# Decode attention block: one head's output weights loaded on 8 partitions, the other seven regrouped, and the last values in two loads

## The chip, the cores and the metric

The kernel runs on one core of one Trainium2 chip. The time is the device time of one execution in microseconds (us). Three runs of the kernel before took 1311.50, 1311.68 and 1311.70 us; their median is 1311.68 us. One more execution was recorded by the hardware profiler and took 1311.62 us, of which its profile spans 1309.6 us from the first instruction to the last; the other 2.0 us lie around that span.

## The reference

One decode step for two sequences (B = 2) of width 512. A layer norm of `x` feeds two branches whose results are multiplied and added to `x`:

```python
xn = _layernorm(x)
q = (xn @ wq).reshape(B, 1, 32, 128)                 # 32 query heads
scores = einsum(q, k) * 128 ** -0.5                  # 8 key/value heads, 4 query heads on each,
o = softmax(scores) @ v                              # 32768 cached positions, all float32
s = o.reshape(B, 1, 4096) @ wo                       # output weights: 4096 x 512
g = silu(relu(xn @ w1 + b1) ** 2 @ w2 + b2)          # 512 -> 1792 -> 512
out = x + s * g
```

The two caches hold 2 x 8 x 32768 x 128 float32 numbers each, 268 MB each. `wq` and `wo` are 8.4 MB each, `w1` and `w2` 3.7 MB each. Everything is read once.

## The kernel before, in words

The 16 streams `s` are the pairs of a key/value head and a sequence (`s = 2 * hkv + b`). For each stream the keys come in two loads of 8 MB (`load_k`, L98) and the values in two loads of 8 MB (`load_v`, L103), each of 64 KB on every one of 128 partitions. Keys live in `kslots`, three slots of 4 MB (L134); values in `vbuf` (L135), 8 MB. Only the last but one value load goes to `kslots`, slots 0 and 1 (L105).

`scores` (L236) turns each quarter of a stream's keys with VectorE's 32x32 transposes into `kt` (L248) and multiplies it on TensorE (L253). `softmax` (L260) and `probs` (L283) make the probabilities `pT`. `values` (L308) multiplies one value load on TensorE into `o_ps` (L316), 32 matmuls of 512 columns, each of which the trace shows as two passes. After a stream's second value load ScalarE copies `o_ps` to `o_sb` (L323), TensorE adds up the four groups and scales (L327), and VectorE writes the four heads' column to `oT` (L328), which holds 128 elements of each head on 128 partitions.

All large loads are issued by SyncE in one fixed order, the list `loads` (L136 to L141). Every entry names the event after which it may be issued (`past`, `give`, `issue`); SyncE's queue is in order, so a load that waits for its buffer holds back all that follow. At the end of the list stand the last two value loads and then the output weights: `load_wo` (L120) fetches `wo` in four groups of eight heads (1024 rows, 2 MB). Partition p gets rows 8p to 8p + 7 of a group, 16 KB in one piece. Groups 0 and 1 go to `kslots` slot 2, groups 2 and 3 to slot 0. The last group comes in four loads, cut by row number on the partition: `PIECES` (L33) gives rows 0 to 3, 4 and 5, 6, and 7, which is 8, 4, 2 and 2 KB on each partition.

For this layout the attention result has to be spread so that partition p holds the elements that meet rows 8p to 8p + 7. For each pair of key/value heads the kernel multiplies `oT` with the selector `sele` on VectorE (`om`, L332), multiplies by the selector `selj` on TensorE (L335), and ScalarE copies the 128x8 result into `oW[:, i, :, b]` (L336). `oW` is kept 32 columns wide, of which two are used.

`project` (L395) then multiplies each row `j` of a group, in four matmuls of 128 columns (one for each quarter of the 512 outputs, on column groups of TensorE), into one accumulator `a_ps`. Its order is group 0, 1, 2, and then the pieces of group 3 (L401 to L404). Two VectorE instructions, the product with `gate` (L406) and the sum with `xe` (L407), and one store for each sequence (L409) end the program.

The work at the start that the change touches: VectorE builds the selectors from the identity with one TENSOR_REDUCE each (L166 to L177), GpSimd clears `oW` (L180), and the layer norm waits for `x` (L190 to L198).

Of the kernel before, what the change touches and what calls it, by code (L numbers as in the profile page):

```python
# [9 lines left out]
F32 = mybir.dt.float32  # L10
AF = mybir.ActivationFunctionType
ALU = mybir.AluOpType
AX = mybir.AxisListType

P = 128
# [12 lines left out]
CHUNK = P * RUN  # L28
# [1 line left out]
TS = (1, 0, 2, 3)  # L30
NT = 4
HALF = 64 * 128
PIECES = ((0, 4), (4, 6), (6, 7), (7, 8))  # L33


@with_exitstack
def gqa_decode_kernel(ctx: ExitStack, tc: tile.TileContext, x, kc, vc, wq, wo, w1, b1, w2, b2, out):
    nc = tc.nc
    B, _, D = x.shape
    _, HKV, SK, DH = kc.shape  # L40
    HQ = wq.shape[1] // DH
# [7 lines left out]
    DE = D // NG  # L49
    WG = 8  # L50
    NWG = HQ // WG
# [6 lines left out]
    const = ctx.enter_context(tc.tile_pool(name="const", bufs=1))  # L58
    ktpool = ctx.enter_context(tc.tile_pool(name="ktpool", bufs=8))
    work = ctx.enter_context(tc.tile_pool(name="work", bufs=2))  # L60
# [3 lines left out]
    def misc(name):  # L64
        return pms.tile([P, 512], F32, tag="ms", name=name)
# [16 lines left out]
    def rows(cache, s):  # L82
        hkv, b = divmod(s, B)
        return cache[b, hkv]
# [17 lines left out]

    def load_v(m):  # L103
        s, u = divmod(m, NCH)
        t = vbuf if m != NV - 2 else kslots[:, 0:2, :].rearrange("p i f -> p (i f)")  # L105
        nc.sync.dma_start(t, rows(vc, s)[u * CHUNK:(u + 1) * CHUNK].rearrange("(p r) d -> p (r d)", p=P))
        return t.rearrange("p (r d) -> p r d", d=DH)
# [9 lines left out]
        return t.rearrange("p (j e) -> p j e", j=FJ)  # L117


    def load_wo(i):  # L120
        if i % 2 == 0:
            wide[i // 2] = kslots[:, 2 - i].rearrange("p (i j e) -> p i j e", i=2, j=WG)
        t = wide[i // 2][:, i % 2]
        src = wo[i * WG * P:(i + 1) * WG * P, :].rearrange("(p j) e -> p j e", p=P)
        if i < NWG - 1:
            nc.sync.dma_start(t, src)
        else:
            for j0, j1 in PIECES:
                nc.sync.dma_start(t[:, j0:j1, :], src[:, j0:j1, :])  # L129
        return t  # L130

    wide = {}
    NK, NV = NS * NT, NS * NCH
    kslots = const.tile([P, 3, HALF], F32, name="kslots")  # L134
    vbuf = const.tile([P, 2 * HALF], F32, name="vbuf")  # L135
    loads = [(None, load_wq, 0), (None, load_half, 0), (None, load_half, 1), (("q", 0), load_w1, 0),  # L136
             (("s", 0), load_half, 2), (None, load_half, 3), (("q", 0), load_w2, 0)]
    for m in range(2, NV):
        loads += [(("s", 2 * m - 2), load_k, m), (("v", m - 3) if m > 2 else ("w", 1), load_v, m - 2)]
    loads += [(("s", NK - 2), load_v, NV - 2), (("v", NV - 3), load_v, NV - 1)]  # L140
    loads += [(("s", NK - 1), load_wo, 0), (("s", NK - 1), load_wo, 1), (("v", NV - 2), load_wo, 2), (("v", NV - 2), load_wo, 3)]  # L141
    past = {None}
    done = [0]

# [6 lines left out]
    def take(f, a):  # L151
        return tiles.pop((f, a))

    def give(*event):
        past.add(event)
        issue()
# [4 lines left out]
    ident = const.tile([P, P], F32, name="ident")  # L161
# [12 lines left out]
    selj = const.tile([P, WG], F32, name="selj")  # L174
    nc.vector.tensor_reduce(selj, ident.rearrange("p (e j) -> p j e", j=WG), axis=AX.X, op=ALU.add)
    sele = const.tile([P, P // WG], F32, name="sele")
    nc.vector.tensor_reduce(sele, ident.rearrange("p (e j) -> p e j", j=WG), axis=AX.X, op=ALU.add)  # L177
    oT = const.tile([P, HQ, B], F32, name="oT")
    oW = const.tile([P, NWG, WG, 32], F32, name="oW")
    nc.gpsimd.memset(oW, 0.0)  # L180
    sc = [pone.tile([P, 512], F32, tag=f"sc{i}", name=f"sc{i}") for i in range(NT)]
    o_ps = [pone.tile([P, 512], F32, tag=f"o{i}", name=f"o_ps{i}") for i in range(2)]
    for t in o_ps:
# [16 lines left out]
    t_ps = misc("xnT_ps")  # L200
# [6 lines left out]
    for d in range(ND):  # L207
        for f in range(2):
            for g in range(NG):
                cc = f * NG + g  # L210
                nc.tensor.matmul(sc[f][32 * g:32 * g + 32, :], xnT[:, d, 0:32], wqt[:, d, cc * 512:(cc + 1) * 512],  # L211
                                 start=(d == 0), stop=(d == ND - 1))
    give("q", 0)
    qT = const.tile([P, B, HKV, REP, 4], F32, name="qT")
    for f in range(2):
        for h in range(REP):
# [3 lines left out]
            t_ps = misc(f"qT_ps{f}_{h}")  # L220
            for e in range(4):
                nc.tensor.transpose(t_ps[:, e * P:(e + 1) * P], qr[:, e].rearrange("p a w -> p (a w)"), ident)  # L222
            v = t_ps.rearrange("p (e g y) -> p g e y", e=4, g=NG)
# [84 lines left out]
    def values(n):  # L308
        s, k = divmod(n, NCH)
        vt = take(load_v, n)  # L310
        o = o_ps[s % 2]
        for c in range(2):
            for i in range(NO // 4):
                for g in range(NG):
                    lo = (c * NG + g) * NO + 4 * i
                    nc.tensor.matmul(o[32 * g:32 * g + 16, :], pT[s][:, k, g, c, 4 * i:4 * i + 4, :].rearrange("p o h -> p (o h)"),  # L316
                                     vt[:, lo:lo + 4, :].rearrange("p o d -> p (o d)"),
                                     start=(k + c + i == 0), stop=(k == NCH - 1 and c == 1 and i == NO // 4 - 1))
        give("v", n)
        if k == NCH - 1:  # L320
            hkv, b = divmod(s, B)
            o_sb = work.tile([P, 512], F32, tag="o_sb", bufs=1, name=f"o_sb{s}")
            nc.scalar.copy(o_sb, o)  # L323
            t_ps = misc(f"oT_ps{s}")
            r4 = rs.pop(s)
            for i in range(4):
                nc.tensor.matmul(t_ps[:, :REP], o_sb[:, i * DH:(i + 1) * DH], r4[:, i, :], start=(i == 0), stop=(i == 3))  # L327
            nc.vector.tensor_copy(oT[:, hkv * REP:(hkv + 1) * REP, b], t_ps[:, :REP])  # L328
            if hkv % 2 == 1:
                i = hkv // 2  # L330
                m = work.tile([P, WG, P // WG], F32, tag="om", bufs=1, name=f"om{s}")
                nc.vector.tensor_mul(m, oT[:, i * WG:(i + 1) * WG, b:b + 1].to_broadcast([P, WG, P // WG]),  # L332
                                     sele[:, None, :].to_broadcast([P, WG, P // WG]))
                t_ps = misc(f"oW_ps{s}")
                nc.tensor.matmul(t_ps[:, :WG], m.rearrange("p h e -> p (h e)"), selj, start=True, stop=True)  # L335
                nc.scalar.copy(oW[:, i, :, b], t_ps[:, :WG])  # L336


# [34 lines left out]
    for n in range(NK):  # L373
        s, i = divmod(n, NT)
        if i == 0:
            set_q(s)
        scores(n)
        if n == 1:
            mlp_up()
        if n == 3:  # L380
            mlp_down()
        if i == 3:
            softmax(s)
        if n >= 5 and n % 2 == 1:
            values((n - 5) // 2)
        if i == 3:
            probs(s)
    values(NV - 2)
    values(NV - 1)


    a_ps = sc[0]
    wot = [take(load_wo, i) for i in range(NWG)]

    def project(i, j0, j1):  # L395
        for j in range(j0, j1):
            for g in range(NG):
                nc.tensor.matmul(a_ps[32 * g:32 * g + 32, :DE], oW[:, i, j, :], wot[i][:, j, g * DE:(g + 1) * DE],
                                 start=(i == 0 and j == 0), stop=(i == NWG - 1 and j == WG - 1))

    for i in range(NWG - 1):  # L401
        project(i, 0, WG)
    for j0, j1 in PIECES:
        project(NWG - 1, j0, j1)  # L404
    asb = work.tile([P, DE], F32, tag="e", bufs=1, name="a_sb")
    nc.vector.tensor_mul(asb, gate, a_ps[:, :DE])  # L406
    nc.vector.tensor_add(xe, asb, xe)  # L407
# [25 lines left out]
```

## Time and profile before

| What | Value |
|---|---|
| median of three runs | 1311.68 us |
| the profiled execution, and its span | 1311.62 us, 1309.6 us |
| mean granted TensorE clock | 0.841 of full speed |
| TensorE matmul busy, 4926 records | 885.4 us, 68% of the span |
| TensorE weight loads busy | 251.1 us, 19% |
| VectorE busy, 742 instructions | 648.8 us, 50% |
| ScalarE, GpSimd busy | 88.3 us, 15.1 us |
| read from HBM | 561.01 MB, 428 GB/s over the span |
| packets on queue q8, kind "instruction" | 38, 0.62 MB |
| last value load landed, as TensorE saw it | 1285.88 us |
| last of the output weights landed | 1305.55 us |

Busy time is summed over an engine's instructions. In the chain that ended last, each step is followed back to what released it, so a transfer that stands there includes its time in the queue. Besides the views, the trace holds one record for every DMA packet, with its start, duration, size and queue, but not which of the core's 16 DMA engines moved it. On one engine a packet starts 3 or 4 ns before the packet ahead of it ends, so the records can be strung into 16 chains. A load on 128 partitions puts eight packets on every chain, followed by one record of 4 bytes, the engine's completion count.

### The profile page before, as it was taken

Reading aid. Unit: us, or ns where it says so; the run is one execution under the profiler, and the core shown is the slowest. Engines: PE = TensorE matmul, PEld = TensorE weight load, DVE = VectorE, ACT = ScalarE, POOL = GpSimd, SP = SyncE. Lnnn points to the kernel's source line nnn. Section 1 sums busy time; section 2 is a strip of 40 time slices with the busy share of each in tenths; the row PEclk is TensorE's granted clock in tenths of the full one; section 3 lists DMA queues with packets and bytes.
Section 4 is the critical chain, followed back from the end, with each engine's and each line's share of the span. In section 5 each row is a group of like instructions: output and inputs, shape, how many; then the busy total and the mean of one; then the engine's idle time right before and its main releaser. Section 6 shows DMA issues by size and latency. Waiting matters only on the chain.

```text
span 1309.6 us, 11506 instructions
## 1 busy us (share of the span) xinstructions
PE 885.4 (68%) x4926; PEld 251.1 (19%) x4926; DVE 648.8 (50%) x742; ACT 88.3 (7%) x237; POOL 15.1 (1%) x76
## 2 busy tenths in 40 slices
PE   3867675658757567775657766566875756776575
PEld 1222121112212111121212211111221211112123
DVE  2855654435555344655435565443655534465410
ACT  0010010101001010000101001010000101000010
POOL 0000000000000000000000000000000000000000
PEclk9988877888878788877789978778987878888788
DMA  9999999999999999999999999999999999999997
GB/s 403 433 441 439 424 439 423 441 433 431 435 427 435 435 427 443 423 439 428 437 429 431 435 427 443 419 443 429 435 435 427 439 427 437 435 425 441 421 441 303
DMA packets 11040, 561.74 MB, mean 429 GB/s; under 512 B 1239, under 2 KB 1259, under 8 KB 1646
## 3 DMA queue, kind: packets, MB, share of 16 engines
q1 hardware_dynamic: 10952, 561.00, 99.2%
q8 instruction: 38, 0.62, 0.2%
q14 instruction: 12, 0.10, 0.0%
q10 hardware_dynamic: 38, 0.02, 0.0%
HBM read 561.01 MB, written 0.00 MB: 428 GB/s over the span
## 4 chain that ended last, share of the span: by engine, by line
DMA 74%; DVE 18%; issue 5%; PE 2%; SPq 0%; DVEq 0%
DMA kslots<-in_A_k_cache 68%; DVE kt L248 18%; DMA kslots<-in_A_wo 2%; DMA kslots<-in_A_v_cache 2%; DMA vbuf<-in_A_wq 2%; PE sc L211 1%; PE o_ps L316 0%; PE h_ps L347 0%; SPq L129 0%; DVE qr L218 0%; DVEq L248 0%; PE qT_ps L222 0%; PE sc L253 0%; DVE h L354 0%; DVE first L355 0%
## 5 line engine op out<-in xcount | busy, mean ns | idle before, releaser
L253 PE MATMUL sc<-kt,qz 128*32 128x512 f32 x2048 | 578.4, 671 | 330.6 <-DVE kt L248 309.0
L248 DVE STREAM_TRANSPOSE kt<-kslots 128x1024 f32<-128x1024 f32 x512 | 580.7, 1205 | 350.9 <-DMA kslots<-in_A_k_cache 350.9
L253 PEld LDWEIGHTS sc<-kt,qz 128*32 128x32 f32 x2048 | 112.0, 115 | 783.1 <-DVE kt L248 580.7
L316 PE MATMUL o_ps<-vbuf,pT 128*16 128x512 f32 x1984 | 228.8, 597 | 11.0 <-DMA vbuf<-in_A_v_cache 11.0
L316 PEld LDWEIGHTS o_ps<-vbuf,pT 128*16 128x16 f32 x1984 | 76.7, 97 | 139.9 <-issue 119.6
L275 ACT ACTIVATE p<-sc,nm 128x512 f32<-128x512 f32 x32 | 23.3, 746 | 991.0 <-DVE nm L271 991.0
L328 DVE COPY oT<-oT_ps 128x4 f32<-128x4 f32 x16 | 2.6, 162 | 121.5 <-PE oT_ps L327 121.5
L258 DVE TENSOR_REDUCE rm<-sc 128x1 f32<-128x512 f32 x32 | 22.1, 691 | 63.9 <-PE sc L253 63.9
L294 ACT COPY pT<-pT_ps 64x256 f32<-64x256 f32 x128 | 46.8, 366 | 19.7 <-PE pT_ps L290 18.2
L300 DVE RECIPROCAL r<-l_ps 128x4 f32<-128x4 f32 x16 | 2.9, 182 | 46.2 <-PE l_ps L298 46.2
L231 POOL COPY qz<-qT 32x16 f32<-32x16 f32 x64 | 12.7, 198 | 1077.4 <-PE sc L253 1042.5
L327 PE MATMUL oT_ps<-rs,o_sb 128*128 128x4 f32 x128 | 16.9, 255 | 11.5 <-ACT o_sb L323 11.4
L290 PE MATMUL pT_ps<-ident,p 128*128 128x128 f32 x128 | 20.2, 309 | 2.9 <-ACT p L275 2.9
L327 PEld LDWEIGHTS oT_ps<-rs,o_sb 128*128 128x128 f32 x128 | 15.5, 191 | 25.6 <-ACT o_sb L323 25.6
L298 PE MATMUL l_ps<-lh,ones 128*128 128x4 f32 x32 | 8.2, 327 | 17.6 <-ACT pT L294 17.6
L290 PEld LDWEIGHTS pT_ps<-ident,p 128*128 128x128 f32 x128 | 17.4, 169 | 3.1 <-ACT p L275 3.1
L323 ACT COPY o_sb<-o_ps 128x512 f32<-128x512 f32 x16 | 9.4, 585 | 100.1 <-PE o_ps L316 100.1
L278 DVE TENSOR_REDUCE l<-l 128x1 f32<-128x2 f32 x16 | 2.5, 155 | 26.9 <-ACT p L275 26.9
L264 PE MATMUL mx_ps<-ident,rm 128*128 128x128 f32 x16 | 5.2, 323 | 14.6 <-DVE rm L262 14.6
L202 PE MATMUL xnT_ps<-ident,xn 128*128 128x128 f32 x4 | 1.1, 428 | 20.4 <-DVE xn L198 20.4
L316 PE MATMUL o_ps<-kslots,pT 128*16 128x512 f32 x64 | 8.4, 682 | 4.2 <-DMA kslots<-in_A_v_cache 4.2
L298 PEld LDWEIGHTS l_ps<-lh,ones 128*128 128x128 f32 x32 | 6.8, 266 | 22.0 <-ACT pT L294 22.0
(68 smaller groups left out, 116.2 us busy)
## 6 DMA issues: line engine op xcount, KB each, us to landing
kslots<-in_A_k_cache SPq DMA_DIRECT2D x4, 4096.0 KB, 20.8
vbuf<-in_B_w SPq DMA_DIRECT2D x2, 3584.0 KB
kslots<-in_A_wo SPq DMA_DIRECT2D x3, 2048.0 KB
kslots<-in_A_wo SPq DMA_DIRECT2D x1, 1024.0 KB
kslots<-in_A_wo SPq DMA_DIRECT2D x1, 512.0 KB
kslots<-in_A_wo SPq DMA_DIRECT2D x2, 256.0 KB, 31.3
vbuf<-in_A_v_cache SPq DMA_DIRECT2D x31, 31.0
kslots<-in_A_k_cache SPq DMA_DIRECT2D x30
```

The costliest lines, as they stand in the source:

```text
L211: nc.tensor.matmul(sc[f][32 * g:32 * g + 32, :], xnT[:, d, 0:32], wqt[:, d, cc * 512:(cc + 1) * 512], start=(d == 0), stop=(d == ND - 1))
L231: nc.gpsimd.tensor_copy(qz[s % 2][32 * a:32 * a + 32, 16:].rearrange("p (e y) -> p e y", e=4)[:, :, a * REP:(a + 1) * REP], qT[32 * a:32 * ...
L248: nc.vector.transpose(r.rearrange("p e o w -> p o e w"), kt[:, g * NO:(g + 1) * NO, e0 * 32:(e0 + 2) * 32].rearrange("p o (e w) -> p o e w ...
L253: nc.tensor.matmul(bank[32 * g:32 * g + 32, :], qz[s % 2][:, lo + 32 * (e0 + e):lo + 32 * (e0 + e) + 32], kts[g][:, e].rearrange("p o w -> ...
L258: nc.vector.tensor_reduce(rm[s][:, u:u + 1], bank, axis=AX.X, op=ALU.max)
L275: nc.scalar.activation(p[:, :, :, u], sc[2 * (s % 2) + u].rearrange("p (o w) -> p o w", w=32), AF.Exp, bias=nm, scale=SCALE, accum_out=l2[ ...
L290: nc.tensor.transpose(t_ps[:, j * P:(j + 1) * P], p[:, o:o + 2].rearrange("p o w u -> p (o w u)"), ident)
L294: nc.scalar.copy(sb[64 * a:64 * a + 64].rearrange("p k g c (i j o) h -> p i o j (g c) k h", i=2, o=2)[:, i, o], v[:, :, :, :, a])
L298: nc.tensor.matmul(t_ps[:, :REP], ones, lh, start=True, stop=True)
L316: nc.tensor.matmul(o[32 * g:32 * g + 16, :], pT[s][:, k, g, c, 4 * i:4 * i + 4, :].rearrange("p o h -> p (o h)"), vt[:, lo:lo + 4, :].rear ...
L323: nc.scalar.copy(o_sb, o)
L327: nc.tensor.matmul(t_ps[:, :REP], o_sb[:, i * DH:(i + 1) * DH], r4[:, i, :], start=(i == 0), stop=(i == 3))
```

## The change

The output weights of the last eight heads are laid out anew. Head 24, the first of them, is taken out of the group and loaded by a new function `load_few` into `few`, 8 partitions of `kslots` slot 1, with 16 rows (32 KB) on each. The source of that load has two outer parts (`y`) of four (`n`) partitions each. Its spread result goes to `oF`, 8 partitions by 16 rows by 16 columns, made when key/value head 6 is finished, and it is multiplied between group 1 and group 2 in 64 matmuls.

The other seven heads come in three loads of 4, 2 and 1 whole heads, where a partition gets 4, 2 or 1 consecutive rows of the piece. Each piece has its own spread, with selectors `sels[nh]` that six new TENSOR_REDUCE instructions build at the start; the piece of one head needs no spread and is copied from `oT`. In the list of loads, `few` stands between `wo` group 1 and group 2. `oW` becomes 16 columns wide instead of 32.

The last value load is split in two, one for the first and one for the second 64 positions of every partition (32 KB packets instead of 64 KB).

```diff
--- before.py
+++ after.py
@@ -30,7 +30,9 @@
 TS = (1, 0, 2, 3)
 NT = 4
 HALF = 64 * 128
-PIECES = ((0, 4), (4, 6), (6, 7), (7, 8))
+
+
+PIECES = ((1, 4), (5, 2), (7, 1))
 
 
 @with_exitstack
@@ -102,6 +104,11 @@
 
     def load_v(m):
         s, u = divmod(m, NCH)
+        if m == NV - 1:
+            for c in range(2):
+                nc.sync.dma_start(vbuf[:, c * HALF:(c + 1) * HALF], rows(vc, s)[u * CHUNK:(u + 1) * CHUNK]
+                                  .rearrange("(p c r) d -> p c (r d)", p=P, c=2)[:, c])
+            return vbuf.rearrange("p (r d) -> p r d", d=DH)
         t = vbuf if m != NV - 2 else kslots[:, 0:2, :].rearrange("p i f -> p (i f)")
         nc.sync.dma_start(t, rows(vc, s)[u * CHUNK:(u + 1) * CHUNK].rearrange("(p r) d -> p (r d)", p=P))
         return t.rearrange("p (r d) -> p r d", d=DH)
@@ -125,20 +134,28 @@
         if i < NWG - 1:
             nc.sync.dma_start(t, src)
         else:
-            for j0, j1 in PIECES:
-                nc.sync.dma_start(t[:, j0:j1, :], src[:, j0:j1, :])
+            base = i * WG * P
+            for h0, nh in PIECES:
+                lo = base + h0 * P
+                nc.sync.dma_start(t[:, h0:h0 + nh, :], wo[lo:lo + nh * P, :].rearrange("(p j) e -> p j e", p=P))
         return t
+
+    def load_few(_):
+        lo = (HQ - WG) * P
+        nc.sync.dma_start(few, wo[lo:lo + P, :].rearrange("(n y j) e -> y n (j e)", y=2, j=16))
 
     wide = {}
     NK, NV = NS * NT, NS * NCH
     kslots = const.tile([P, 3, HALF], F32, name="kslots")
+    few = kslots[0:8, 1, :]
     vbuf = const.tile([P, 2 * HALF], F32, name="vbuf")
     loads = [(None, load_wq, 0), (None, load_half, 0), (None, load_half, 1), (("q", 0), load_w1, 0),
              (("s", 0), load_half, 2), (None, load_half, 3), (("q", 0), load_w2, 0)]
     for m in range(2, NV):
         loads += [(("s", 2 * m - 2), load_k, m), (("v", m - 3) if m > 2 else ("w", 1), load_v, m - 2)]
     loads += [(("s", NK - 2), load_v, NV - 2), (("v", NV - 3), load_v, NV - 1)]
-    loads += [(("s", NK - 1), load_wo, 0), (("s", NK - 1), load_wo, 1), (("v", NV - 2), load_wo, 2), (("v", NV - 2), load_wo, 3)]
+    loads += [(("s", NK - 1), load_wo, 0), (("s", NK - 1), load_wo, 1), (("v", NV - 2), load_few, 0), (None, load_wo, 2),
+              (None, load_wo, 3)]
     past = {None}
     done = [0]
 
@@ -175,9 +192,16 @@
     nc.vector.tensor_reduce(selj, ident.rearrange("p (e j) -> p j e", j=WG), axis=AX.X, op=ALU.add)
     sele = const.tile([P, P // WG], F32, name="sele")
     nc.vector.tensor_reduce(sele, ident.rearrange("p (e j) -> p e j", j=WG), axis=AX.X, op=ALU.add)
+    sels = {}
+    for nh in (16, 4, 2):
+        sels[nh] = const.tile([P, P // nh + nh], F32, name=f"sel_{nh}")
+        nc.vector.tensor_reduce(sels[nh][:, 0:P // nh], ident.rearrange("p (e j) -> p e j", j=nh), axis=AX.X, op=ALU.add)
+        nc.vector.tensor_reduce(sels[nh][:, P // nh:], ident.rearrange("p (e j) -> p j e", j=nh), axis=AX.X, op=ALU.add)
     oT = const.tile([P, HQ, B], F32, name="oT")
-    oW = const.tile([P, NWG, WG, 32], F32, name="oW")
+    oW = const.tile([P, NWG, WG, 16], F32, name="oW")
     nc.gpsimd.memset(oW, 0.0)
+    oF = const.tile([8, 16, 16], F32, name="oF")
+    nc.gpsimd.memset(oF, 0.0)
     sc = [pone.tile([P, 512], F32, tag=f"sc{i}", name=f"sc{i}") for i in range(NT)]
     o_ps = [pone.tile([P, 512], F32, tag=f"o{i}", name=f"o_ps{i}") for i in range(2)]
     for t in o_ps:
@@ -326,13 +350,31 @@
             for i in range(4):
                 nc.tensor.matmul(t_ps[:, :REP], o_sb[:, i * DH:(i + 1) * DH], r4[:, i, :], start=(i == 0), stop=(i == 3))
             nc.vector.tensor_copy(oT[:, hkv * REP:(hkv + 1) * REP, b], t_ps[:, :REP])
-            if hkv % 2 == 1:
-                i = hkv // 2
-                m = work.tile([P, WG, P // WG], F32, tag="om", bufs=1, name=f"om{s}")
-                nc.vector.tensor_mul(m, oT[:, i * WG:(i + 1) * WG, b:b + 1].to_broadcast([P, WG, P // WG]),
-                                     sele[:, None, :].to_broadcast([P, WG, P // WG]))
-                t_ps = misc(f"oW_ps{s}")
-                nc.tensor.matmul(t_ps[:, :WG], m.rearrange("p h e -> p (h e)"), selj, start=True, stop=True)
+            i = hkv // 2
+            t_ps = misc(f"oW_ps{s}")
+
+            def spread(h0, nh, se, sj, x0):
+                m = work.tile([P, P], F32, tag="om", bufs=1, name=f"om{s}_{h0}")
+                nc.vector.tensor_mul(m.rearrange("p (h e) -> p h e", h=nh),
+                                     oT[:, h0:h0 + nh, b:b + 1].to_broadcast([P, nh, P // nh]),
+                                     se[:, None, :].to_broadcast([P, nh, P // nh]))
+                nc.tensor.matmul(t_ps[:, x0:x0 + nh], m, sj, start=True, stop=True)
+
+            if hkv == HKV - 2:
+                m = work.tile([P, P], F32, tag="om", bufs=1, name=f"om{s}")
+                nc.vector.tensor_mul(m[:, 0:8].rearrange("p (y n) -> p y n", y=2),
+                                     oT[:, i * WG:i * WG + 1, b:b + 1].to_broadcast([P, 2, 4]),
+                                     sels[16][:, 0:8].rearrange("p (n y) -> p y n", y=2))
+                nc.tensor.matmul(t_ps[0:8, 0:16], m[:, 0:8], sels[16][:, 8:], start=True, stop=True)
+                nc.scalar.copy(oF[:, :, b], t_ps[0:8, 0:16])
+            elif hkv == HKV - 1:
+                for h0, nh in PIECES[:-1]:
+                    spread(i * WG + h0, nh, sels[nh][:, 0:P // nh], sels[nh][:, P // nh:], h0)
+                h0 = PIECES[-1][0]
+                nc.scalar.copy(oW[:, i, 1:h0, b], t_ps[:, 1:h0])
+                nc.vector.tensor_copy(oW[:, i, h0, b:b + 1], oT[:, i * WG + h0, b:b + 1])
+            elif hkv % 2 == 1:
+                spread(i * WG, WG, sele, selj, 0)
                 nc.scalar.copy(oW[:, i, :, b], t_ps[:, :WG])
 
 
@@ -392,16 +434,18 @@
     a_ps = sc[0]
     wot = [take(load_wo, i) for i in range(NWG)]
 
-    def project(i, j0, j1):
+    def project(ow, wt, j0, j1, start=False, stop=False):
         for j in range(j0, j1):
             for g in range(NG):
-                nc.tensor.matmul(a_ps[32 * g:32 * g + 32, :DE], oW[:, i, j, :], wot[i][:, j, g * DE:(g + 1) * DE],
-                                 start=(i == 0 and j == 0), stop=(i == NWG - 1 and j == WG - 1))
+                nc.tensor.matmul(a_ps[32 * g:32 * g + 16, :DE], ow[:, j, :], wt[:, j, g * DE:(g + 1) * DE],
+                                 start=start and j == j0, stop=stop and j == j1 - 1)
 
     for i in range(NWG - 1):
-        project(i, 0, WG)
-    for j0, j1 in PIECES:
-        project(NWG - 1, j0, j1)
+        project(oW[:, i], wot[i], 0, WG, start=(i == 0))
+        if i == 1:
+            project(oF, few.rearrange("p (j e) -> p j e", j=16), 0, 16)
+    for h0, nh in PIECES:
+        project(oW[:, NWG - 1], wot[NWG - 1], h0, h0 + nh, stop=(h0 + nh == WG))
     asb = work.tile([P, DE], F32, tag="e", bufs=1, name="a_sb")
     nc.vector.tensor_mul(asb, gate, a_ps[:, :DE])
     nc.vector.tensor_add(xe, asb, xe)
```

## The prediction

> **What bounds the kernel now.** I read the page first: slices, queues and chain.
>
> ```profile
> span 1309.6 us, 11506 instructions
> ...
> DMA  9999999999999999999999999999999999999997
> ...
> q1 hardware_dynamic: 10952, 561.00, 99.2%
> q8 instruction: 38, 0.62, 0.2%
> ```
>
> The DMA engines are full in every slice but the last, so time can only be won from what the busiest engine still has to do, or after its last byte. Next, the chain of waits in order of time, at its end:
>
> ```profile
> 1274.05 31.46 DMA kslots<-in_A_wo
> ...
> 1305.55 0.47 PE sc L398 x8
> ...
> 1306.04 0.30 DVE a_sb L406
> ...
> 1306.36 0.29 DVE xe L407
> ```
>
> The last piece of `wo` lands at 1305.55; a fixed tail of 0.47 + 0.30 + 0.29 us and the store follow. The windows of 1 us show how the engines run out:
>
> ```profile
> 1296.00:1297.00 1.00, 1.00 (x22) 0.98 (x24) 0.30 (x2) 0.00 (x0) 0.00 (x0) 1.00 1.04 430
> ...
> 1298.00:1299.00 1.00, 1.00 (x45) 1.00 (x40) 0.00 (x0) 0.00 (x0) 0.00 (x0) 1.00 0.70 279
> 1299.00:1300.00 1.00, 1.00 (x47) 1.00 (x40) 0.00 (x0) 0.00 (x0) 0.00 (x0) 1.00 0.47 197
> ...
> 1303.00:1304.00 1.00, 0.90 (x32) 0.84 (x32) 0.00 (x0) 0.00 (x0) 0.00 (x0) 1.00 0.46 174
> 1304.00:1305.00 1.00, 0.92 (x28) 0.47 (x24) 0.00 (x0) 0.00 (x0) 0.00 (x0) 1.00 0.34 131
> ```
>
> The last two columns are the DMA share and GB/s: from 1298 on about half the engines have nothing left, seven microseconds ahead of the others. The packet records say why. Strung into 16 chains, the last value load is finished by seven chains at 1278.64 to 1279.59, by four at 1283.98 to 1284.08 and by five at 1285.62 to 1285.88. Eight chains carry the 38 packets of q8, in a fixed turn: those with four by then are the middle ones, those with five late. Each such packet (16,384 B, median 1.07 us) also lengthens the data packet after it, by 0.48 us (2.90 against 2.42), so it costs its chain 1.55 us. The fifth late chain has no q8 packet but seven gaps of 0.31 us, each before a packet some 0.65 us longer. The late chains run without a gap to the end: they are the bound.
>
> Which chains get `few`? The start-up loads of two rows (`x`, `xe`) put their packets on only two chains, neither of which ever carries q8. They finish the last value load at 1279.29 and 1279.59, and the last piece of `wo` at 1298.9 and 1299.33: 6.2 us ahead of the last chain.
>
> **The change part by part**, against the profiled execution (1309.6 us of span + 2.0; 1311.62 is 0.06 below the median of 1311.68).
>
> *Bytes taken from the late engines.* Now each chain moves the last group as eight packets each of 8, 4, 2 and 2 KB. On the last chain group 2 ends at 1300.54 and the pieces at 1303.01, 1304.26, 1304.91 and 1305.55. The new pieces are 4, 2 and 1 heads: packets of 8, 4 and 2 KB. One piece of 0.64 us is gone: the last lands at 1304.91. **-0.64 us.**
>
> *Bytes given to two engines.* `few` is 256 KB in 8 packets of 32 KB; its source is two times four. I take it that it runs on two engines, as the two-row loads do, four packets on each: 4 x 1.21 us (32 KB packet, median) = 4.84 us. The later of the two, 1299.33 now, ends at 1299.33 + 4.84 - 0.64 = 1303.5, still 1.4 us ahead of 1304.91. **0** on the path. The bounds: 0 if the two are those chains, +4.84 - 0.64 = +4.20 if a late chain gets it.
>
> *Last values in two loads.* Eight packets of 32 KB and their completion take 9.69 us at the start (completions at 22.11, 31.80); twice that is 19.38 against 19.35 for one load of 64 KB packets (1266.53 to 1285.88): **+0.03 us**. SP issues one more load; `wo` groups 0 and 1 follow 0.4 us later:
>
> ```profile
> 1256.35 0.33 SPq L106 DMA_DIRECT2D vbuf<-in_A_v_cache  x1
> 1256.73 15.10 SPq L126 DMA_DIRECT2D kslots<-in_A_wo  x3
> 1271.88 2.61 SPq L129 DMA_DIRECT2D kslots<-in_A_wo  x4
> ...
> 1285.88 8.92 PE L316 MATMUL o_ps<-vbuf,pT 128*16 128x512 f32 x64 [10.98 <-DMA vbuf<-in_A_v_cache]
> ```
>
> The first chain reaches group 0 at 1278.64, so 22 us cover that. The second value half needs no new buffer, so SP does not wait between the halves. TensorE now starts half of these 64 passes at about 1276.2 and ends the rest some 3.4 us earlier than 1294.8. Nothing on the path gains: group 0 lands at 1290.77.
>
> *`few` in SP's queue.* It goes to slot 1, which TensorE reads until 1274.9 (the end of the other value load's passes), where slot 0 was free at 1271.58. Behind it `wo` group 2 and the three pieces are issued 3.7 us later, by 1278.5 or so. The first chain gets to group 2's place at 1288.4: 10 us of cover. Without it the early engines would wait, and they have 6 us to lose. SP issues one load more in all (+1 values, +1 `few`, -1 piece) at 0.33 to 1.16 us.
>
> *TensorE.* Projection grows from 128 matmuls (256 passes) to 96 + 64 + 28 = 188 (376 passes). The trace has 64 passes of group 2 in 1.69 us, 26.4 ns each. Group 1 lands at 1295.65; from there 64 + 128 (`few`) + 64 + 32 + 16 + 8 passes take 312 x 26.4 = 8.24 us, to 1303.9. That is 1.0 us before the last piece lands. The first engines deliver `few` by about 1294.2, ahead of group 1. So **0**, but with that little cover (a rival below).
>
> *Spreads.* Streams 12 and 13 get a small product, matmul and ScalarE copy, streams 14 and 15 a second product and matmul (0.30 us DVE, 0.39 us PE, as the old ones); only stream 15's are late. In the trace before they end at 1297.95; now some 3 us earlier, and pieces wait until 1303. **0.**
>
> *Start.* Six more TENSOR_REDUCE at 0.28 to 0.37 us, 2.1 us in all, can fall into VectorE's chain before `xn`, as the old four did:
>
> ```profile
> 18.57 0.37 DVE L166 TENSOR_REDUCE selh<-ident 128x4 f32<-128x128 f32 x1
> ...
> 19.61 0.16 DVE L197 RECIPROCAL st<-st 128x1 f32<-128x1 f32 x1
> ...
> 23.00 8.91 PE L211 MATMUL sc<-vbuf,first 128*32 128x512 f32 x64 [1.46 <-DMA vbuf<-in_A_wq]
> ...
> 28.50 0.33 SPq L111 DMA_DIRECT2D vbuf<-in_B_w  x1
> ...
> 45.67 0.80 SPq L96 DMA_DIRECT2D kslots<-in_A_k_cache  x2
> ```
>
> The first projection would start up to 1.4 us later, and so the two issues. The first chain runs out of work at 41.5 and at 49.98: 4.3 us of cover is left, **0**. GpSimd's two memsets gate nothing there.
>
> *Instruction packets.* 240 records more in the projection and 16 in spreads, on TensorE alone: 11506 / 38 = 303 instructions a packet, so about one packet more, near the end. In their turn the three after 1272 fall on middle chains. Such a hit moves a middle chain from 1303.7 to 1305.3 now, 1304.6 then: still before 1304.91. **0.**
>
> Sum: -0.64 + 0.03 = **-0.61 us**, 1311.68 to **1311.1**.
>
> **The rivals.**
>
> *A. A load on few engines holds up the queue (slower).* If the packets of `few` fall on late chains, or the loads behind it wait for it, the last landing moves by +4.84 - 0.64 + 0.03 = +4.2: **1315.9**. It decides from the point where the two chains' lead falls under 4.2 us. For it: SP's queue is one, and 8 partitions are a sixteenth of a load. Against: chains run up to 7 us apart, across several loads. [...] No run here yet shows a large load on two engines.
>
> *B. TensorE becomes the bound of the tail.* It has 1.0 us of cover, 1.5 with the last piece's 0.47. The granted clock fell to 0.5 for 10.24 us from 1279.96, after 5 us of idleness. With the values in two parts there are new idle stretches, at 1280 to 1285.9 and just before 1295.65. One step of 3.41 us at half clock costs 1.7 us: the tail ends 0.25 us later than DMA sets it, **1311.3**; two steps give 1313.0. Against: in the trace before, the same stretch from 1290.2 kept full clock with similar gaps. [...]
>
> *C. The load is not split over two engines.* All eight packets on one chain: 8 x 1.21 = 9.68 us, it ends at 1298.9 - 0.64 + 9.68 = 1307.9, 2.4 us after today's last: **1314.1**.
>
> *D. A q8 packet more on a late chain.* The turn shifts by two: +1.55 - 0.61, **1312.6**.
>
> **How the numbers follow.** 0.2% (2.6 us) is about what a measurement of this kernel can tell from no change. Chances: forecast 0.66 (1310.8 to 1311.3), B 0.12, D 0.07, A 0.08, C 0.04, and 0.03 for a little more gain: the chain behind the last ends at 1305.3 to 1305.4, so not much below 1310.7. Only A is outside 0.2%: slower 0.08, faster 0.01, within 0.91. The range holds forecast, B and D: 1310.5 to 1312.7.
>
> **What would show it.** Right: the last `wo` landing near 1304.9 with 0.47 us of TensorE behind it; a DMA share in the last microseconds one or two engines higher; `few` landed before group 1; three q8 packets after 1272. Wrong: TensorE busy when the last piece lands (B); the last landing near 1309.8 (A) or 1308 (C); gaps in the late chains after 1256.

## The result, and the profile after

The changed kernel is slower: 1314.84 us median of 11 runs (1313.95 to 1315.62) against 1311.58 us of the kernel before (1311.31 to 1311.84), a ratio of 1.0025 with a 95% interval of 1.0015 to 1.0034. That is +3.26 us where -0.61 us was forecast. The profiled execution spans 1312.8 us (before 1309.6).

The chain of waits of the changed kernel, in order of time, at its end (start and length in us, then what the chain follows):

```profile
1285.81 6.00 PE o_ps L340 x32
...
1295.52 6.85 PE sc L440 x212
1302.36 0.93 issue
1303.30 5.87 PE sc L440 x122
1309.16 0.02 issue
1309.18 0.30 DVE a_sb L450
```

Before, the last link ahead of the fixed tail was a landing of `wo`. Now no DMA stands in the chain after 1285.8: TensorE works from the second half of the last values to 1309.16 and sets the end. Of the passes that L440 makes, the 212 are the rest of groups 0 and 1 and 126 of head 24's 128; the 122 are the last two of head 24, group 2 and the pieces.

The stretches of that tail, cut by hand. Each line has the stretch and its length; the busy time and the instructions of TensorE's matmuls, its weight loads, VectorE, ScalarE and GpSimd; the granted TensorE clock, the DMA share and GB/s:

```profile
1294.40:1297.80 3.40, 3.40 (x100) 3.10 (x100) 0.29 (x1) 0.17 (x1) 0.00 (x0) 1.00 0.98 403
1297.80:1301.20 3.40, 3.40 (x122) 3.18 (x116) 0.00 (x0) 0.00 (x0) 0.00 (x0) 0.94 0.69 287
1301.20:1303.30 2.10, 1.17 (x23) 0.59 (x15) 0.00 (x0) 0.00 (x0) 0.00 (x0) 0.50 0.56 222
1303.30:1308.00 4.70, 4.70 (x90) 3.52 (x94) 0.00 (x0) 0.00 (x0) 0.00 (x0) 0.54 0.11 39
1308.00:1309.20 1.20, 1.10 (x44) 0.81 (x32) 0.02 (x1) 0.00 (x0) 0.00 (x0) 1.00 0.00 0
```

Three things are to be seen. In the second line TensorE is busy without a break, with head 24's passes, and at the end of it the clock falls to 0.5, where it stays for 6.83 us by the clock records. In the third it stands still: the last pass before the gap and the first one behind it start 1.35 us apart, of which the chain counts 0.93 as "issue", a wait for nothing that the profile shows. In the last two the DMA engines have almost nothing left: by the trace's record of landings the last piece of `wo` lands at 1304.88 (before 1305.50), and TensorE works on for over four microseconds.

The queue of instructions has one packet more, as forecast:

```profile
span 1312.8 us, 11779 instructions
...
q8 instruction: 39, 0.64, 0.2%
```

### The profile page after: what moved, and what is told of

Its sections match the earlier page's. It is cut to its first block, busy times and chain, and to the rows that moved or that the text cites. A ratio compares the mean times of both kernels' runs of the same rounds, so it can differ in the third digit from the quotient of the medians.

```text
span 1312.8 us, 11779 instructions
## 1 busy us (share of the span) xinstructions
PE 894.4 (68%) x5054; PEld 257.3 (20%) x5054; DVE 651.3 (50%) x754; ACT 88.5 (7%) x239; POOL 14.9 (1%) x77
## 4 chain that ended last, share of the span: by engine, by line
DMA 71%; DVE 20%; issue 5%; PE 4%; DVEq 0%; ACTq 0%; ACT 0%
DMA kslots<-in_A_k_cache 68%; DVE kt L272 19%; DMA vbuf<-in_A_v_cache 2%; PE sc L440 1%; DMA first<-in_A_x 1%; PE o_ps L340 1%; PE sc L235 1%; PE sc L277 0%; PE h_ps L389 0%; DVE qr L242 0%; DVEq L272 0%; PE qT_ps L246 0%; PE xnT_ps L226 0%; PE oT_ps L351 0%; DVE h L396 0%
## 6 DMA issues: line engine op xcount, KB each, us to landing
kslots<-in_A_wo SPq DMA_DIRECT2D x1, 1024.0 KB, 26.4
```

## The experiments

Three theories were put against each other. "Clock": passes over 8 of 128 rows make the granted clock fall. "Work": 128 more passes and their instructions are too many at any clock. "DMA": the load on two engines, or the later issues, delay the stream. Beside each group of runs the kernel before was timed on the same chip; its medians were 1311.54, 1311.62 and 1311.64 us.

### Head 24 loaded, but not multiplied

```diff
-        if i == 1:
-            project(oF, few.rearrange("p (j e) -> p j e", j=16), 0, 16)
```

> The changed kernel without the 64 matmuls of the eight-partition head; its load and everything else stay. Left out: head 24's part of the output. Theory 'clock' (passes over 8 rows leave most of TensorE unused, the granted clock falls, and the tail runs at half speed) and theory 'work' (128 more passes and their instructions are too many at any clock) both expect the forecast gain of the DMA side: the last output weights at about 1304.9 and 1311.0 us, 0.6 below the kernel before. Theory 'DMA' (the load on two engines or the later issues delay the stream) expects no change from the changed kernel: 1314.8.

Measured: 1311.21 us (1310.83 to 1311.68, 10 runs) against 1311.54; ratio 0.9998 (0.9988 to 1.0007). The whole loss is gone though the two-engine load still runs, so the "DMA" theory falls. The 64 matmuls cost 1314.84 - 1311.21 = 3.6 us. What is left is -0.33 us, the sign of the forecast gain and half its size; the interval of the ratio contains 1. The end hangs on landings again:

```profile
1278.47 26.04 DMA kslots<-in_A_wo
...
1304.55 1.09 PE sc L440 x24
```

The chain puts the 24 passes of the last two pieces together. By the trace's records the last piece lands at 1305.14 and the last eight passes start at 1305.18, 0.27 us behind the sixteen before them, so the last landing sets the end here too. From the landing of the last values to this one it takes 19.00 us, where it took 19.66 before: the gain of the bytes is there. The last values landed 0.30 us later than before (1286.14 and 1285.84), which takes half of it away; why they did is not shown.

### Head 24 multiplied over 128 partitions

```diff
-    oF = const.tile([8, 16, 16], F32, name="oF")
+    oF = const.tile([P, 16, 16], F32, name="oF")
...
-                nc.scalar.copy(oF[:, :, b], t_ps[0:8, 0:16])
+                nc.scalar.copy(oF[0:8, :, b], t_ps[0:8, 0:16])
...
-            project(oF, few.rearrange("p (j e) -> p j e", j=16), 0, 16)
+            project(oF, kslots[:, 1, :].rearrange("p (j e) -> p j e", j=16), 0, 16)
```

> The changed kernel, but head 24's 64 matmuls go over all 128 partitions, with zeros as weights on 120 of them: the same number of passes, columns and instructions. 'Clock' expects the clock to stay at 1.0 until the end, so that only the wait of about 1.4 us in the middle of these passes stays: 312 passes x 26.7 ns + 1.4 from 1295.5 end near 1305.5 to 1306.3, and the time is 1311.2 to 1312.2. 'Work' expects 1314.8 as in the changed kernel.

Measured: 1312.47 us (1312.27 to 1313.03, 10 runs); ratio 1.0007 (0.9998 to 1.0017). Stretches of this kernel's tail, same columns:

```profile
1298.30:1302.20 3.90, 3.88 (x140) 3.60 (x130) 0.00 (x0) 0.00 (x0) 0.00 (x0) 1.00 0.67 277
1302.20:1303.40 1.20, 0.00 (x0) 0.00 (x0) 0.00 (x0) 0.00 (x0) 0.00 (x0) 1.00 0.47 191
1303.40:1307.10 3.70, 3.67 (x122) 3.37 (x122) 0.00 (x0) 0.00 (x0) 0.00 (x0) 1.00 0.15 56
```

And the end of its chain of waits:

```profile
1296.18 6.00 PE sc L440 x212
1302.18 1.22 issue
1303.41 3.68 PE sc L440 x122
```

The same passes in the same order, only wider, and the clock stays at 1.0; the last 122 passes take 3.68 us where they took 5.87. The clock is worth 1314.84 - 1312.47 = 2.4 us of the loss. The standstill stays (1.22 us of "issue"), and the time is 0.3 us above the range that "clock" gave. What the standstill and the 128 passes cost at full clock is the theory "work", and it keeps the rest: 1312.47 - 1311.21 = 1.26 us. The last piece landed at 1305.56 in this kernel, no earlier than before, but TensorE ended 1.5 us behind it.

### The last values in two loads, alone

```diff
+        if m == NV - 1:
+            for c in range(2):
+                nc.sync.dma_start(vbuf[:, c * HALF:(c + 1) * HALF], rows(vc, s)[u * CHUNK:(u + 1) * CHUNK]
+                                  .rearrange("(p c r) d -> p c (r d)", p=P, c=2)[:, c])
+            return vbuf.rearrange("p (r d) -> p r d", d=DH)
```

> The kernel before with only the last value load in two parts. By the chain of packets it costs 0.03 us, and nothing at the end waits for TensorE: 1311.6, the same as before within 0.2. If the two loads or the idle time between their two halves on TensorE were the cause of the loss, some 3 us more.

Measured: 1311.57 us (1311.30 to 1312.09, 10 runs) against 1311.54; ratio 1.0000 (0.9991 to 1.0010). As forecast, no cost or gain shows where the landing sets the end:

```profile
1276.42 29.30 DMA kslots<-in_A_wo
...
1305.76 0.47 PE sc L403 x8
```

### The last values in one load again, the rest as changed

The lines just shown are taken out of the changed kernel.

> The changed kernel with the last values in one load again. TensorE then starts on the output weights about 3 us later. If the tail is bound by TensorE ('clock' and 'work'), it ends later by up to as much: 1315.5 to 1318. If the two value loads took part in the loss, or TensorE did not bound the tail, 1314.8 or less.

Measured: 1316.51 us (1316.00 to 1318.34, 4 runs); ratio 1.0040 (1.0025 to 1.0055). So the split had been saving 1.7 us between the medians, though the four runs here lie 2.3 us apart: with TensorE as the bound, its start counts. The standstill and slow passes are both there; here the clock was at half for one step, from 1305.98 to 1309.40:

```profile
1298.22 5.91 PE sc L435 x204
1304.12 0.93 issue
1305.05 5.50 PE sc L435 x122
```

### The extra passes in the kernel before, over 8 and over 128 rows

```diff
     for i in range(NWG - 1):
         project(i, 0, WG)
+        if i == 1:
+            for j in range(16):
+                for g in range(NG):
+                    nc.tensor.matmul(a_ps[32 * g:32 * g + 16, :DE], oW[0:8, 1, j % WG, 0:16],
+                                     wot[1][0:8, j % WG, g * DE:(g + 1) * DE], start=False, stop=False)
```

The second kernel has 128 for 8 in both slices.

> The kernel before, with none of the change's loads or layouts, and 64 matmuls more between group 1 and group 2: eight rows, 16 weight columns, 128 columns, part of group 1's weights once more on 8 partitions. The output has that part twice. TensorE is through with group 1 at about 1300.3; 128 passes at 26.7 ns and one wait for instructions of 1.4 us bring the end to about 1308.6 where it was 1306.0: 'work' expects 1314.2, in this kernel and in the one with 128 rows. 'Clock' expects the granted clock to fall within or after these passes and 1315.5 to 1317.

> The same as the run with eight rows, but the 64 extra matmuls go over 128 partitions (the output has part of group 1 twice). 'Clock' expects full clock to the end and 1314.2, at least 1.3 us less than with eight rows. 'Work' expects the same time as with eight rows.

Measured: 1316.88 us with 8 rows (1315.71 to 1317.92, 4 runs; ratio 1.0040, 1.0025 to 1.0055) and 1314.87 us with 128 (1314.02 to 1316.64, 8 runs; ratio 1.0026, 1.0015 to 1.0036). Stretches of the kernel with 8 rows and then of the one with 128, each with two lines of its chain of waits:

```profile
1300.10:1303.60 3.50, 3.50 (x124) 3.41 (x128) 0.00 (x0) 0.00 (x0) 0.00 (x0) 0.92 0.56 228
1303.60:1305.60 2.00, 1.19 (x18) 0.33 (x11) 0.00 (x0) 0.00 (x0) 0.00 (x0) 0.50 0.24 93
1305.60:1310.40 4.80, 4.79 (x100) 4.79 (x103) 0.00 (x0) 0.00 (x0) 0.00 (x0) 0.55 0.01 3
...
1304.79 0.82 issue
1305.61 5.73 PE sc L398 x122
```

```profile
1300.00:1303.60 3.60, 3.60 (x134) 3.49 (x128) 0.00 (x0) 0.00 (x0) 0.00 (x0) 1.00 0.56 228
1303.60:1305.70 2.10, 0.14 (x9) 0.02 (x4) 0.00 (x0) 0.00 (x0) 0.00 (x0) 1.00 0.23 90
1305.70:1309.40 3.70, 3.63 (x122) 3.36 (x121) 0.03 (x1) 0.00 (x0) 0.00 (x0) 1.00 0.02 4
...
1303.72 1.96 issue
1305.68 3.67 PE sc L398 x122
```

Without any of the change's loads or layouts the clock falls after 3 us of eight-row passes, and not after as many full ones. The difference of the medians is 2.0 us, though the ranges overlap by one run: 1316.64 with 128 rows, where the other seven end at 1315.11 or below. Both kernels leave the standstill at the same time, 1305.61 and 1305.68; the whole difference lies in the same 122 passes behind it, 5.73 us at half clock for most of them against 3.67 us. The 128-row kernel is 0.7 us above what was expected: its standstill lasted 1.96 us, not 1.4.

### The standstill, moved

This is the kernel with head 24 over 128 partitions and 32 small matmuls at the start:

```diff
     xnT = first[:, 2].rearrange("p (d b) -> p d b", d=ND)
+    d_ps = misc("d_ps")
+    for _ in range(32):
+        nc.tensor.matmul(d_ps[:, :4], ident, selh, start=True, stop=True)
     t_ps = misc("xnT_ps")
```

> The changed kernel with head 24 multiplied over 128 partitions, and 32 small matmuls (128 instructions, 64 passes) more on TensorE at the very start, where it waits. There the tail has a wait of about 1.4 us after 126 of the 128 extra passes. If it is a wait for instructions, which come in blocks, it comes 64 passes earlier, at about 1300.3, and the packets of the instruction queue come earlier by 1.7 us; the time stays near 1312.5. If the wait belongs to that place in the work (a landing, a buffer), it stays at the 126th pass.

Measured: 1321.35 us (1320.80 to 1322.19, 4 runs). The time was missed: the 64 small passes took 13.8 us, not a few, and held the first projection back to 34.2 us (23.2 in the changed kernel). The second pair of key loads was then issued at 56.8 us, after the DMA engines had run dry between 50 and 53, and everything behind it came some 8.6 us later, the landings too. The place of the standstill answers the question all the same. Its chain of waits:

```profile
1304.26 3.68 PE sc L443 x126
1307.94 1.20 issue
1309.14 3.69 PE sc L443 x128
1312.83 0.86 issue
1313.69 1.92 PE sc L443 x58
```

The first 126 passes here are 64 of group 1 and 62 of head 24: the wait comes after 62 of its passes where it came after 126. It moved by exactly the 64 passes that were put in 1.3 ms earlier, and the next one follows 128 passes, that is 256 TensorE instructions, behind it. It goes by the count of instructions, not by a landing or a buffer. At each of the seven standstills in the traces of the experiments and the changed kernel, TensorE goes on 1.25 to 1.48 us after a packet of the instruction queue ends in the packet records: here 1307.74 and 1309.14, then 1312.21 and 1313.69; in the changed kernel 1301.88 and 1303.30. (Landings, too, are recorded some 0.4 us after their packets end.)

### Head 24 ahead of the last values

```diff
-            wide[i // 2] = kslots[:, 2 - i].rearrange("p (i j e) -> p i j e", i=2, j=WG)
+            wide[i // 2] = kslots[:, i // 2].rearrange("p (i j e) -> p i j e", i=2, j=WG)
...
-    few = kslots[0:8, 1, :]
+    few = kslots[0:8, 2, :]
...
-    loads += [(("s", NK - 2), load_v, NV - 2), (("v", NV - 3), load_v, NV - 1)]
-    loads += [(("s", NK - 1), load_wo, 0), (("s", NK - 1), load_wo, 1), (("v", NV - 2), load_few, 0), (None, load_wo, 2),
-              (None, load_wo, 3)]
+    loads += [(("s", NK - 2), load_v, NV - 2), (("s", NK - 1), load_few, 0), (("v", NV - 3), load_v, NV - 1)]
+    loads += [(("v", NV - 2), load_wo, i) for i in range(NWG)]
...
     values(NV - 2)
+    project(oF, few.rearrange("p (j e) -> p j e", j=16), 0, 16, start=True)
     values(NV - 1)
...
-        if i == 1:
-            project(oF, few.rearrange("p (j e) -> p j e", j=16), 0, 16)
```

> The changed kernel with head 24's weights loaded ahead of the last value load (into slot 2; the other groups move to slots 0 and 1) and multiplied between the two last value loads, where TensorE waits. 'Clock' and 'work' expect the 128 passes to cost nothing there: 1311.0, faster than before by 0.6. 'DMA' expects 1314.8, since the same load runs on the same two engines.

Measured: 1311.39 us (1310.91 to 1312.19, 10 runs) against 1311.54; ratio 1.0000 (0.9990 to 1.0009). The loss is gone, but of the gain of 0.6 only 0.15 shows. Stretches before the end:

```profile
1297.00:1300.40 3.40, 0.78 (x31) 0.50 (x20) 0.00 (x0) 0.00 (x0) 0.00 (x0) 0.95 0.71 299
1300.40:1303.90 3.50, 3.17 (x68) 2.60 (x72) 0.00 (x0) 0.00 (x0) 0.00 (x0) 0.56 0.62 247
```

With the values in two parts TensorE is early, waits for group 2, and after this nearly empty stretch runs the next 3.4 us at half clock. The same wait, 2.9 us long, left the clock at 1.0 in the kernel without head 24's passes and in the one with the split alone, so this step need not come. Whether the split costs time here is not shown. It was taken out:

> Head 24's weights loaded and multiplied ahead of the last value load, and that load in one part again. In the run with both the early head and the split, TensorE sat idle for 2.94 us before group 2, the granted clock fell to 0.5 for one step of 3.4 us there, and the tail was TensorE's. Without the split TensorE is still busy with groups 0 and 1 until about 1300.3, so the clock stays at 1.0 and the last landing sets the end: 'clock' expects the whole forecast gain, 1311.0, 0.4 to 0.6 below the kernel before. If the gain of the bytes were never there, 1311.5 or more.

Measured: 1311.13 us (1310.96 to 1311.65, 11 runs) against 1311.64 (1311.33 to 1312.02, 18 runs): -0.51 us; ratio 0.9997 (0.9988 to 1.0006). Eight of its eleven runs are below the fastest of the kernel before; the interval still contains 1. It is the fastest version by its median, though the ranges with and without the split overlap and the two profiled executions took 1311.21 and 1311.24 us. The end hangs on landings again (the last at 1305.19), with the passes at full clock:

```profile
1276.38 28.18 DMA kslots<-in_A_wo
...
1304.61 1.08 PE sc L429 x24
```

### Two heads on four engines

```diff
-PIECES = ((1, 4), (5, 2), (7, 1))
+PIECES = ((2, 4), (6, 1), (7, 1))
...
-    few = kslots[0:8, 2, :]
+    few = kslots[0:16, 2, :]
...
-        nc.sync.dma_start(few, wo[lo:lo + P, :].rearrange("(n y j) e -> y n (j e)", y=2, j=16))
+        nc.sync.dma_start(few, wo[lo:lo + 2 * P, :].rearrange("(n y j) e -> y n (j e)", y=4, j=16))
```

This is the last kernel with a second head taken out. The spread is written for two heads; the last two heads need none.

> The same with two heads (24 and 25) on 16 partitions, 16 rows each, in a load of four times 4 partitions, and the other six in pieces of 4, 1 and 1 heads. Every DMA engine loses 32 KB and, if the load runs on four engines, each of those gains 128 KB. If all four are ahead of the last by over 3.6 us, the gain doubles: 1310.3 to 1310.5. If one of the two new engines is a late one, it ends some 3.6 us after the others do now: 1314 to 1315.

Measured: 1315.08 us (1314.88 to 1315.36, 8 runs) against 1311.64; ratio 1.0026 (1.0016 to 1.0037). Single microseconds near the end:

```profile
1303.00:1304.00 1.00, 1.00 (x48) 1.00 (x41) 0.00 (x0) 0.00 (x0) 0.00 (x0) 1.00 0.31 119
1306.00:1307.00 1.00, 1.00 (x44) 0.89 (x34) 0.00 (x0) 0.00 (x0) 0.00 (x0) 1.00 0.06 25
1308.00:1309.00 1.00, 1.00 (x42) 0.81 (x34) 0.00 (x0) 0.00 (x0) 0.00 (x0) 1.00 0.03 12
```

From 1305.4 on the DMA share is about one sixteenth, one engine, until the last piece lands at 1308.94; the last value load, too, landed at 1290.57 and not at 1285.84 as before, 4.7 us later, about the 4.84 us that four packets of 32 KB were reckoned to take on an engine. So at least one of the engines that this load uses has no lead. Which one it is the runs don't show.

## Why the prediction was wrong

**The step that failed** is the one on TensorE: 312 passes x 26.4 ns from group 1's landing to 1303.9, put at 0 on the path with 1.0 us of cover. The passes ran from 1295.5 to 1309.16. The term was mis-sized twice. The rate of 26.4 ns holds at full clock only (in this tail four passes begin every 109 ns there, every 213 ns at half clock), and half clock lasted 6.83 us: 2.4 us by the run with 128 rows. The other part is the standstill of 1.35 us and the 128 passes themselves, as far as they reach past the last landing: 1.26 us, which the runs don't divide further. Together 3.6 us, less the 0.33 that is left of the gain: +3.3. One execution of each kernel was profiled; the eleven runs of the changed kernel lie 1.7 us apart, where those of the kernel before lie within 0.5, so the length of the slow stretch may differ between executions.

**Rival B** had the right bound and the wrong cause. It looked for idle stretches. After the one of 1280 to 1285.8 the second value half did start at half clock, but the clock was back at 1.0 at 1290.52, before the projection. It fell again at 1300.76, in the middle of a stretch that the profile shows as wholly busy. (The half clock in the profile before lasted from 1279.45 to 1289.69 by the clock records, half a microsecond earlier than B put it.) B's two slow steps gave 1313.0; with the standstill of 1.35 us, which it did not have, that makes 1314.4. Its chance was put at 0.12. Busy time alone does not separate these tails: 2.8 and 3.0 us of unbroken passes with 8 rows ended at a clock of 0.5, 3.9 and 3.6 us with 128 rows at 1.0. By these runs rows count too. The weights of 120 of the 128 rows were zeros in one of these kernels.

**The standstill** was not among the costs: the prediction asked only what a packet of q8 does to the data, not whether TensorE would stand still for one. In the tail 256 TensorE instructions (128 passes and their weight loads) last 3.4 us, against some 34 us from packet to packet over the span. That the packet then comes too late is the reading that fits the runs. In the profile before, every wait in the tail that is as long ends with a landing or with another engine's result. The prediction also divided all engines' instructions by the packets, 303 to one; TensorE's own records alone are 9852, 259 to one, and 256 more of them brought one packet more. In these tails the standstill lasted 0.8 to 2.0 us.

**What held.** The bytes: last landing 0.62 us earlier (forecast 0.64). Counted from the landing of the last values, which itself moves by some 0.4 us between kernels, it came 0.55 us earlier, and 0.65 to 0.68 in five of the experiments with this layout; with head 24 over 128 partitions it did not, and why stays open. `few` on two chains with a lead: in the packet records of the changed kernel two chains carry 20 packets of 32 KB from 1257 on and the other fourteen 16, and the last landing was far from A's 1309.8 and C's 1308, and the run with four engines shows the price where a lead is missing. The split: 0.03 us forecast, 0.03 between the medians, far inside the spread of the runs. `few` in SP's queue: issued at 1275.29 and the rest by 1278, without effect. One more q8 packet, and the last landing shows no late chain hit (D fell). The start: projection from 23.2, key loads at 46.2, no loss; but the cover was smaller than the 4.3 us written, since in the run that overran it the first data packet starts 1.0 us after the issue in the packet records.

## What to carry to other kernels

When bytes are moved off the busiest DMA engine, look at what the new layout asks of the engine behind it: here a tile on 8 partitions took as many TensorE passes as one on 128 (128 in both runs), and 2.8 us of such passes were followed by 6.83 us at half clock. Put them where TensorE has time (here between the last two value loads), or, for the clock alone, give them all rows with zeros. A cover of one microsecond computed from a rate is none until the clock and the standstills of that stretch are known.

## What the runs showed of the hardware

- Busy time alone did not set the granted clock. It fell to 0.5 after 2.8 and 3.0 us of eight-row passes in two kernels (the changed one, and the one before with eight-row passes added), and in the one without the split 5.5 us after the first of them and past the standstill. It stayed at 1.0 with 128 rows in three (head 24 over 128 partitions, with and without the shift, and the one before with such passes added), through standstills of up to 1.96 us. How the clock is decided is not shown.
- The packets of the instruction queue have 16 KB each, one for some 259 TensorE instructions; two standstills in one kernel lie 256 instructions apart. In a burst of passes at some 27 ns TensorE stood for 0.8 to 2.0 us; the place moved with the count of instructions, and it went on 1.25 to 1.48 us after a packet's end. That it waits for the instructions in that packet is the reading that fits all seven cases.
- By the packet records before, the 38 instruction packets lie on eight of the sixteen chains in a fixed turn and cost their chain 1.55 us each. That is the larger part of why chains that carry equal bytes end the last value load up to 7.2 us apart (one more chain had seven gaps of its own), and how much can be shifted between them depends on which of them a small load takes: two had 6.2 us of lead, and of those that the larger load used at least one had none (the last values landed 4.7 us later).
